# Decayed linear attention and a channel mix on one core: attention in sub-chunks of 64 tokens on 64x64 matmul tiles

## The chip, the cores and the metric

The kernel runs on one of the eight cores of a Trainium2 chip. The metric is the time of one execution on the device in microseconds (us). Before the change three runs gave 405.16, 406.31 and 408.67, median 406.31.

## The reference

Two layers follow each other, all in fp32. The first is linear attention with a decay for each feature, for 4 batches, 8 heads, 768 tokens and 48 features a head. The second is a channel mix: it blends each token with the one before, squares a ReLU, and multiplies by a sigmoid gate.

```python
for t in range(S):                       # attention, for every batch and head
    state = alpha[t, :, None] * state + outer(k[t], v[t])     # 48 x 48
    y[t] = q[t] @ state
x = y of all heads side by side          # 768 tokens x 384 features a batch
xk = mu_k * x + (1 - mu_k) * x_prev      # x_prev: the token before
xr = mu_r * x + (1 - mu_r) * x_prev
out = sigmoid(xr @ w_r) * (max(xk @ w_k, 0) ** 2 @ w_v)       # 384 -> 1024 -> 384
```

## The kernel before

**Groups and chunks.** The 3072 tokens are cut into chunks of 128 (`C`) and the chunks into nine groups: three groups of two chunks for batch 0, then two of three for each later batch. Heads go in four pairs (`NP`); a pair has its features on partitions 0 to 47 and 64 to 111. The decay is taken out of the recurrence: `prep_p` (line 227) runs the products of alpha as a scan (`pp`), and `prep_gh` (line 243) multiplies `q` by them, scans alpha backwards (`al`, line 254), and multiplies `k` by that. What is left is causal attention without decay: inside a chunk a masked product, across chunks a state of 48x48 a head.

**Attention of a chunk** (`attn`, line 281) is a list of pieces, each with a weight. For each pair, `scores` (line 318) makes k times q for the two heads of 128 tokens by 128, two matmuls on 48 partitions each; VectorE multiplies all eight by the mask into `am` (line 329, 1024 columns). `trans` (line 339) transposes k, ScalarE copies it out (`ht`). `both` runs `intra` (v times `am`, lines 384 and 391, two matmuls with 64 and 48 output partitions for a pair) and `update` (line 349, the state's growth, 48x48 for each head), and `inter` (line 407, old state times q, one 112x112 block-diagonal matmul a pair) adds to the same PSUM tile. The new state is the old one plus `pu` (line 357). ScalarE copies the outputs to `xt` and those of the last pair to `x3` (lines 416, 417), and two DMAs (line 420) spread them over the 16 free partitions beside each of the other three pairs' heads. Group 0 does without these DMAs (`direct`, line 403).

**The channel mix of a group**: `mix` (lines 460 to 470) makes xk and xr and splits each into a high part that a float32r matmul takes whole and a low rest. `moe` has three stages: up (line 487, 72 matmuls of three kinds: high times high, high times low, low times high), gate (line 512), and down (line 527). After up, ScalarE and VectorE make the ReLU, its square and the square's low part (lines 495 to 501). The weights are split in the same way while the first groups run (`split`).

**The order of work.** The streams of TensorE and SyncE are written out by hand; those of the other engines follow a scheduler's estimate and are then fixed. `merge` (line 46) puts the pieces of the next group's attention between the matmuls of this group's channel mix, by weight, so that the attention ends about 12 units (`LEAD`) before the mix does. A piece with no work (`pad`, `sp`) only spaces the others. In the first two groups, `PARAM["pos"]` says at which piece each weight split and each `prep` is issued, and 19 pieces of the attention of group 1 go ahead of the first up matmuls.

## Time and profile before

| what | value |
|---|---|
| three runs, median | 405.16, 406.31, 408.67; 406.31 us |
| the profiled execution, first to last instruction | 407.4 us |
| mean granted TensorE clock | 0.955 |
| busy: TensorE, VectorE, ScalarE, GpSimd | 371.3, 284.6, 190.8, 69.7 us |
| matmul records | 2834 |
| first up matmul of group 0 | 40.7 us |
| first up matmul of group 2 | 106.4 us |
| first up matmul of group 8, the last | 370.2 us |

The engines are PE (TensorE's matmuls), PEld (its weight loads), DVE (VectorE), ACT (ScalarE), POOL (GpSimd) and SP (SyncE). An fp32 matmul leaves two records, each with a weight load of its own; a float32r matmul and a transpose leave one. A stage below is the time from the first up matmul of a group to that of the next one: it holds the group's channel mix and the next group's attention.

### The profile page before, as it was taken

How to read it: one execution, taken by the hardware profiler on the slowest of the kernel's cores; microseconds unless marked ns; L12 is line 12 of the kernel's file. 1: busy time of each engine (PE TensorE's matmuls, PEld its weight loads, DVE VectorE, ACT ScalarE, POOL GpSimd, SP SyncE). 2: the span in 40 equal slices, each digit the busy share in tenths (PEclk: the TensorE clock that was granted, in tenths of full speed). 3: DMA queues.
4: the chain of work that ended last, by engine and by line, in shares of the span. 5: the costliest groups of instructions: out<-in, count | busy, mean ns of one | idle time of the engine just before them, and what ended most of it. 6: DMA issues, size and time to landing. Idle time of an engine off the chain costs nothing. (4 is left out here: it accounts for less than half of the span.)

```text
span 407.4 us, 7186 instructions
## 1 busy us (share of the span) xinstructions
PE 371.3 (91%) x2834; PEld 337.1 (83%) x2834; DVE 284.6 (70%) x451; ACT 190.8 (47%) x421; POOL 69.7 (17%) x85
## 2 busy tenths in 40 slices
PE   7665988898889999999989999999999999999993
PEld 6545877788779878898869978899889978999992
DVE  5899999995995699529972399809982654337510
ACT  3457864545644573327433273526634634345500
POOL 5364374250030004000400004000400000000000
PEclk9695998699999999999969999999999999999998
DMA  8994188336016212251023410251000100011001
GB/s 214 284 392 176 24 250 223 105 102 180 30 45 196 59 39 70 71 165 42 2 68 114 125 39 2 69 150 43 18 2 12 43 21 0 2 36 39 2 20 45
DMA packets 15816, 35.82 MB, mean 88 GB/s; under 512 B 1568, under 2 KB 9440, under 8 KB 15776
## 3 DMA queue, kind: packets, MB, share of 16 engines
q1 hardware_dynamic: 14608, 34.21, 27.7%
q10 hardware_dynamic: 1168, 1.09, 1.1%
q8 instruction: 24, 0.39, 0.4%
q14 instruction: 16, 0.13, 0.1%
HBM read 29.49 MB, written 4.72 MB: 84 GB/s over the span
## 5 line engine op out<-in xcount | busy, mean ns | idle before, releaser
L495 ACT ACTIVATE r<-pk 128x384 f32<-128x384 f32 (+1 forms) x72 | 32.2, 452 | 79.9 <-PE pk L487 49.1
L527 PE MATMUL pv<-wvl,kh 128*128 128x384 f32 x192 | 65.5, 341 | 2.9 <-DVE wvl L195 2.9
L527 PE MATMUL pv<-wvh,kl 128*128 128x384 f32 x192 | 65.6, 341 | 1.2 <-DVE kl L501 1.2
L527 PE MATMUL pv<-wvh,kh 128*128 128x384 f32 x192 | 65.2, 339 | 0.0
L318 PE MATMUL sp<-q,k 48*128 48x128 f32 x384 | 43.9, 332 | 18.4 <-DVE am L329 12.1
L318 PEld LDWEIGHTS sp<-q,k 48*128 48x128 f32 x384 | 29.8, 204 | 34.6 <-DVE am L329 14.6
L487 PE MATMUL pk<-xkh,wkh 128*128 128x384 f32 (+1 forms) x216 | 50.1, 339 | 2.1 <-ACT xkh L468 1.8
L487 PE MATMUL pk<-xkh,wkl 128*128 128x384 f32 (+1 forms) x216 | 50.0, 341 | 0.0
L501 DVE TENSOR_TENSOR kl<-k,kh 128x384 fp32r<-128x384 f32 (+1 forms) x72 | 45.7, 635 | 6.1 <-ACT kh L500 2.0
L487 PE MATMUL pk<-xkl,wkh 128*128 128x384 f32 (+1 forms) x216 | 49.5, 338 | 0.0
L460 ACT ACTIVATE x<-xt,mu 128x384 f32<-128x384 f32 (+1 forms) x54 | 29.4, 576 | 29.2 <-DMA xt<-x 21.6
L499 DVE TENSOR_TENSOR k<-r 128x384 f32<-128x384 f32 (+1 forms) x56 | 29.9, 534 | 17.8 <-ACT r L495 16.3
L254 DVE TENSOR_TENSOR_SCAN al<-al 112x383 f32<-112x383 f32 (+1 forms) x36 | 41.3, 1185 | 0.3
L249 DVE TENSOR_TENSOR q<-q,pp 112x768 f32<-112x768 f32 (+1 forms) x20 | 16.1, 808 | 36.3 <-DMA q<-q_p 36.3
L257 POOL TENSOR_TENSOR k<-k,al 112x768 f32<-112x768 f32 (+1 forms) x18 | 30.7, 1704 | 62.5 <-DVE al L254 46.1
L487 PEld LDWEIGHTS pk<-xkh,wkh 128*128 128x128 f32 x216 | 35.5, 195 | 4.9 <-ACT xkh L468 2.3
L527 PEld LDWEIGHTS pv<-wvl,kh 128*128 128x128 f32 x192 | 36.6, 190 | 3.2 <-DVE wvl L195 3.2
L527 PEld LDWEIGHTS pv<-wvh,kl 128*128 128x128 f32 x192 | 36.5, 190 | 1.8 <-DVE kl L501 1.8
L487 PEld LDWEIGHTS pk<-xkl,wkh 128*128 128x128 f32 x216 | 35.6, 194 | 2.8 <-issue 0.6
L487 PEld LDWEIGHTS pk<-xkh,wkl 128*128 128x128 f32 x216 | 35.2, 194 | 2.7 <-issue 0.2
L527 PEld LDWEIGHTS pv<-wvh,kh 128*128 128x128 f32 x192 | 36.6, 191 | 0.2 <-ACT wvh L192 0.2
L532 DVE TENSOR_TENSOR sig<-pv,sig 128x384 f32<-128x384 f32 x24 | 13.3, 554 | 33.3 <-ACT x L460 16.7
(93 smaller groups left out, 591.9 us busy)
## 6 DMA issues: line engine op xcount, KB each, us to landing
out<-sig SPq DMA_DIRECT2D x24, 192.0 KB, 1.8
k<-k_p SPq DMA_DIRECT2D x6, 672.0 KB, 4.6
al<-al_p SPq DMA_DIRECT2D x6, 672.0 KB, 4.8
q<-q_p SPq DMA_DIRECT2D x6, 672.0 KB, 6.6
v<-v_p SPq DMA_DIRECT2D x6, 672.0 KB, 5.3
wkraw<-wk_p SPq DMA_DIRECT2D x4, 768.0 KB, 14.2
vraw<-wv_p SPq DMA_DIRECT2D x4, 768.0 KB, 8.7
v<-v_p SPq DMA_DIRECT2D x3, 448.0 KB, 8.3
```

The lines of the kernel that those rows point to most:

```text
L249: (DVE if PARAM["g"][min(g, 2)][p] == "D" else POOL).tensor_tensor(q[:, hp], q[:, hp], pp[:, hp], op=ALU.mult)
L254: DVE.tensor_tensor_scan(back, back, back, initial=al[:, i, n : n + 1], op0=ALU.mult, op1=ALU.bypass)
L257: (DVE if PARAM["h"][min(g, 2)][p] == "D" else POOL).tensor_tensor(k[:, hp], k[:, hp], al[:, hp, 1:], op=ALU.mult)
L318: PE.matmul(sp[c][:, j, p, :], h[r0 : r0 + D, p, c * C : (c + 1) * C], q[r0 : r0 + D, p, c * C : (c + 1) * C], start=True, stop=True,)
L460: ACT.activation(x, xt[:, t, 1 : 1 + n], AF.Copy, scale=mu[:, i, t : t + 1])
L487: PE.matmul(pk, w[:, t, cols], x[:, t], start=part == 0 and t == 0, stop=part == 2 and t == NT - 1,)
L495: ACT.activation(r, pk, AF.Relu)
L499: DVE.tensor_tensor(k2, r, r, op=ALU.mult)
L501: DVE.tensor_tensor(kl[:, f], k2, kh[:, f].bitcast(F32), op=ALU.subtract)
L527: PE.matmul(pv, x[:, f, cols], w[:, f], start=f == 0 and i == 0, stop=f == NF - 1 and i == 2,)
L532: DVE.tensor_tensor(sig[t], pv, sig[t], op=ALU.mult)
```

## The change

Each chunk of 128 tokens is cut into two sub-chunks of 64 (`s`), and the state is kept at the start of each. Every product of the attention becomes a matmul with at most 64 partitions in and at most 64 out, so that it takes one quarter of the 128x128 array, and four neighbours in the stream always take the four different quarters:

- `scores`: 16 matmuls of 64 tokens by 64 (before 8 of 128 by 128); the mask has 512 columns instead of 1024.
- `intra`: 16 of 64 by 64 (before 8).
- `inter`: 16 (before 4). Those that land in the quarter's own half go to `yu`; the others (`cross`) go to `sp`, and `leave` adds them on VectorE (two adds of 128 columns a chunk, new).
- `update`: 16 with 48 columns (before 8). VectorE makes two states a chunk (`advance`, 192 columns each; before one state in two halves).

All of a chunk that can go together is one uninterrupted run (`visit`): the update of the next chunk, intra and inter of this one, and the scores of the next. A group of three chunks has four visits: update and scores; twice all four; intra and inter. The transposes stay separate pieces, ahead of each visit. `sp` and `yu` are single PSUM tiles of two banks each. The state is dense (192 columns) and goes round five buffers. The product with the carried scale is on VectorE for all groups (before on GpSimd for the first two). Group 0 uses the two DMAs as well. The table of positions becomes a short list (`FILL`), and the attention of group 1 goes wholly beside the channel mix of group 0. `prep` of a later group goes to the start of the attention's pieces. The layout of `v` on the host loses its padding, and the order of heads in the output is permuted with the weights.

The diff, cut to its core (what it removes of `attn` is in the listing above):

```diff
+HC = C // 2
+VW = H * D + HB - D
...
+PAD = 3.0
...
+FILL = [
+    ("wr0", 2), ("pp1", 4), ("wr1", 6), ("prep10", 8), ("prep11", 9), ("wv0", 11),
+    ("prep12", 13), ("prep13", 14), ("wv1", 17), ("load2", 18), ("wv2", 24), ("wv3", 28), ("pp2", 32),
+    ("prep20", 34), ("prep21", 36), ("prep22", 38), ("prep23", 40),
+]
...
+    none, *rings = (cp.tile([R, NP * D + HB - D], F32, name=f"st{i}") for i in range(5))
...
-        v = p2.tile([C, nck, NP, R], F32, tag="v", name=f"v{g}")
+        v = p2.tile([C, nck, VW], F32, tag="v", name=f"v{g}")
...
+        xt = p2.tile([128, NT + 1, 1 + n], F32, tag="xt", name=f"xt{g}")
...
+        sides = [(s, j) for s in range(2) for j in range(2)]
+        quads = [(o, j) for o in range(2) for j in range(2)]
...
+        def trans(c):
+            pt = ps.tile([C, NP, R], F32, tag="pt", name=f"pt{g}_{c}")
+            for p in range(NP):
+                need(f"prep{g}{p}")
+                PE.transpose(pt[:, p, :], h[:, p, c * C : (c + 1) * C], ident[:R, :R])
+            ht[c] = p2.tile([C, NP, R], F32, tag="ht", name=f"ht{g}_{c}")
+            ACT.copy(ht[c], pt)
+
+        def scores(c):
+            for p in range(NP):
+                need(f"prep{g}{p}")
+                for s, j in sides:
+                    rr = slice(j * HB, j * HB + D)
+                    t0 = c * C + s * HC
+                    PE.matmul(
+                        sp[c - 1][s * HC : (s + 1) * HC, j, p * HC : (p + 1) * HC],
+                        h[rr, p, t0 : t0 + HC], q[rr, p, t0 : t0 + HC],
+                        start=True, stop=True,
+                    )
+            am[c] = p2.tile([C, 2, NP, HC], F32, tag="am", name=f"am{g}_{c}")
+            DVE.tensor_tensor(
+                am[c], sp[c - 1][:, :, : NP * HC].rearrange("c j (p t) -> c j p t", p=NP),
+                mask.unsqueeze(1).unsqueeze(1).to_broadcast([C, 2, NP, HC]), op=ALU.mult,
+            )
+
+        def intra(c, opened):
+            for a in range(2):
+                for j in range(2):
+                    for s in range(2):
+                        for o in range(2):
+                            p = 2 * a + o
+                            e0 = (2 * p + j) * D
+                            i = 2 * a + j
+                            PE.matmul(
+                                yu[c][o * HB : (o + 1) * HB, s, i * HC : (i + 1) * HC],
+                                v[s * HC : (s + 1) * HC, c, e0 : e0 + HB],
+                                am[c][s * HC : (s + 1) * HC, j, p, :],
+                                start=i == 0 and s not in opened, stop=False, skip_group_check=True,
+                            )
+
+        def inter(c, cross):
+            for a in range(2):
+                for o, j in quads:
+                    p, s, i = 2 * a + o, j ^ cross, 2 * a + j
+                    rr = slice(j * HB, j * HB + D)
+                    t0 = c * C + s * HC
+                    oo = slice(o * HB, o * HB + (HB if cross else D))
+                    if cross:
+                        out_ = sp[c][oo, j, (NP + a) * HC : (NP + a + 1) * HC]
+                    else:
+                        out_ = yu[c][oo, s, i * HC : (i + 1) * HC]
+                    PE.matmul(
+                        out_, before[c, s][rr, p * D : p * D + (HB if cross else D)], q[rr, p, t0 : t0 + HC],
+                        start=bool(cross), stop=True, skip_group_check=True,
+                    )
+
+        def grown(c):
+            return yu[c - 1][:, :, NP * HC : NP * (HC + D)].rearrange("r s (p e) -> r s p e", p=NP)
+
+        def update(c, opened):
+            u = grown(c)
+            for p in range(NP):
+                for s, j in sides:
+                    if s not in opened:
+                        continue
+                    e0 = (2 * p + j) * D
+                    r0, r1 = j * HB, HB + j * D
+                    PE.matmul(
+                        u[r0:r1, s, p, :],
+                        ht[c][s * HC : (s + 1) * HC, p, r0:r1],
+                        v[s * HC : (s + 1) * HC, c, e0 : e0 + D],
+                        start=p == 0, stop=True, skip_group_check=True,
+                    )
+
+        def advance(c):
+            u = grown(c)
+            old = state.get(b, none)
+            before[c, 0] = old
+            new = before[c, 1] = fresh()
+            DVE.tensor_tensor(by_pair(new), by_pair(old), u[:R, 0], op=ALU.add)
+            if final and c == nck - 1:
+                return
+            nxt = state[b] = fresh()
+            DVE.tensor_tensor(by_pair(nxt), by_pair(new), u[:R, 1], op=ALU.add)
+            if c == nck - 1:
+                DVE.tensor_tensor(
+                    by_pair(nxt), by_pair(nxt),
+                    pscl[:R, g * NP : (g + 1) * NP].unsqueeze(2).to_broadcast([R, NP, D]),
+                    op=ALU.mult,
+                )
+
+        def leave(c):
+            x = xt[:, :, 1 + c * C : 1 + (c + 1) * C]
+            ACT.copy(
+                x[:R].rearrange("r i (s t) -> r i s t", s=2),
+                yu[c][:R, :, : NP * HC].rearrange("r s (i t) -> r i s t", i=NP),
+            )
+            for s in range(2):
+                part = x[:R, 1 - s :: 2, s * HC : (s + 1) * HC]
+                DVE.tensor_tensor(
+                    part, part,
+                    sp[c][:R, 1 - s, NP * HC : (NP + 2) * HC].rearrange("r (a t) -> r a t", a=2),
+                    op=ALU.add,
+                )
+            if c == nck - 1:
+                for o in range(2):
+                    (nc.sync if g == 0 else nc.scalar).dma_start(
+                        xt[o * HB + D : (o + 1) * HB, :NT, 1:], xt[o * HB : o * HB + D, NT, 1:]
+                    )
+
+        def visit(c):
+            more = c + 1 < nck
+            sp[c] = ps.tile([128, 2, 512], F32, tag="sp", name=f"sp{g}_{c}")
+            yu[c] = ps.tile([128, 2, 512], F32, tag="yu", name=f"yu{g}_{c}")
+            opened = ()
+            if more:
+                opened = (0,) if final and c + 2 == nck else (0, 1)
+                update(c + 1, opened)
+            if c >= 0:
+                intra(c, opened)
+                inter(c, 0)
+                inter(c, 1)
+            if more:
+                scores(c + 1)
+                advance(c + 1)
+            if c >= 0:
+                leave(c)
+
+        pieces = [(0.0, start), (0.4, lambda: trans(0)), (PAD, lambda: None)]
+        for c in range(-1, nck):
+            if c >= 0 and c + 1 < nck:
+                pieces += [(PAD, lambda: None), (0.4, lambda c=c: trans(c + 1)), (PAD, lambda: None)]
+            elif c >= 0:
+                pieces += [(2 * PAD, lambda: None)]
+            pieces.append((1.2 + 1.2 * (0 <= c < nck - 1), lambda c=c: visit(c)))
+        return pieces
...
-        for _, f in tick(attn(0)):
+        for i, (_, f) in enumerate(attn(0)):
             f()
+            if i == 3:
+                need("wk0")
+        need("wk1")
...
-                    side.insert(int(len(side) * PA["prep"]), (0.0, lambda: prep(g + 2)))
+                    side.insert(1, (0.0, lambda: prep(g + 2)))
...
-                    for _, f in side[: PA["a1"]] + main[: PA["hold"]]:
+                    for _, f in main[:HOLD]:
                         f()
-                    main, side = main[PA["hold"] :], side[PA["a1"] :]
+                    main = main[HOLD:]
```

**TensorE, group 4's channel mix with the attention of group 5.** `pk` is up, `sp` scores, `pt` the transposes. Before, from the first up matmul:

```order
L487 MATMUL pk<-xkh,wkh 128x384 x3
L318 MATMUL sp_0_1981<-q_1545,k_1544 128x128 x4
L487 MATMUL pk<-xkh,wkl 128x384 x3
L318 MATMUL sp_0_1981<-q_1545,k_1544 128x128 x2
L487 MATMUL pk<-xkl,wkh 128x384 x3
L318 MATMUL sp_0_1981<-q_1545,k_1544 128x128 x2
L339 MATMUL pt_0_2004<-ident,k_1544 128x112
L487 MATMUL pk<-xkh,wkh 128x384 x3
L339 MATMUL pt_0_2004<-ident,k_1544 128x112 x3
L487 MATMUL pk<-xkh,wkl 128x384 x3
L487 MATMUL pk<-xkl,wkh 128x384 x3
L487 MATMUL pk<-xkh,wkh 128x384 x3
```

After, from the end of the second visit on:

```order
L346 MATMUL sp_0_2570<-q_1885,k_1884 64x64 x16
L500 MATMUL pk<-xkh,wkh 128x384 x3
L500 MATMUL pk<-xkh,wkl 128x384 x3
L500 MATMUL pk<-xkl,wkh 128x384 x3
L500 MATMUL pk<-xkh,wkh 128x384 x3
L500 MATMUL pk<-xkh,wkl 128x384 x3
L500 MATMUL pk<-xkl,wkh 128x384 x3
L336 MATMUL pt_2_2675<-ident,k_1884 128x112 x4
L500 MATMUL pk<-xkh,wkh 128x384 x3
L500 MATMUL pk<-xkh,wkl 128x384 x3
L500 MATMUL pk<-xkl,wkh 128x384 x3
L500 MATMUL pk<-xkh,wkh 128x384 x3
```

The scores stood in pieces of two or four matmuls between threes of up; now they come as one block of 16 at the end of a visit, and up runs unbroken but for the transposes until the next one.

**VectorE, in the same stage.** `am` is the mask, `k` and `kl` the square and its low part, `al` the backward scan for a later group, `st` the state, `xt` the adds of `leave`. Before, near the stage's start:

```order
L235 RECIPROCAL al_2414<-pp_2415 112x4
L329 TENSOR_TENSOR am_0_2002<-sp_0_1981,mask 128x1024
L499 TENSOR_TENSOR k_1995<-r 128x384
L254 SCALAR_TENSOR_TENSOR al_1971<-al_1971 112x383
L501 TENSOR_TENSOR kl<-k_1995,kh 128x384
L254 SCALAR_TENSOR_TENSOR al_1971<-al_1971 112x383 x3
L499 TENSOR_TENSOR k_2041<-r 128x384
L501 TENSOR_TENSOR kl<-k_2041,kh 128x384
L499 TENSOR_TENSOR k_2057<-r 128x384
L501 TENSOR_TENSOR kl<-k_2057,kh 128x384
L329 TENSOR_TENSOR am_1_2087<-sp_1_2062,mask 128x1024
```

After, around the last two visits:

```order
L411 TENSOR_TENSOR st_107<-st_106,yu_1_2703 112x192
L415 TENSOR_TENSOR st_104<-st_107,yu_1_2703 112x192
L417 TENSOR_TENSOR st_104<-st_104,pscl 112x192
L352 TENSOR_TENSOR am_2_2768<-sp_1_2702,mask 128x512
L431 TENSOR_TENSOR xt_2424<-xt_2424,sp_1_2702 112x2x64 x2
L512 TENSOR_TENSOR k_2783<-r 128x384
L281 SCALAR_TENSOR_TENSOR al_2985<-al_2985 112x383
L514 TENSOR_TENSOR kl<-k_2783,kh 128x384
L281 SCALAR_TENSOR_TENSOR al_2985<-al_2985 112x383 x3
L431 TENSOR_TENSOR xt_2424<-xt_2424,sp_2_2816 112x2x64 x2
L276 TENSOR_TENSOR q_2988<-q_2988,pp_2986 112x768
L545 TENSOR_TENSOR sig<-pv,sig 128x384
```

The four scans stood among the first masks and squares of the stage; now they stand after the last mask, ahead of the last visit's two adds into `xt`.

## Prediction on record

> **What bounds the kernel now.** I read the page's busy times first, then the windows cut at the first up matmul of each group, then the chain of waits inside a clean stage.
>
> ```profile
> PE 371.3 (91%) x2834; PEld 337.1 (83%) x2834; DVE 284.6 (70%) x451; ACT 190.8 (47%) x421; POOL 69.7 (17%) x85
> ```
>
> PE is busy 91% of the span, but the windows show two regimes. Columns: window, length, then busy time (instructions) of PE, PEld, DVE, ACT, POOL, the granted clock, DMA.
>
> ```profile
> 0.00:40.70 40.70, 26.40 (x252) 22.96 (x253) 34.06 (x50) 20.23 (x38) 20.86 (x38) 0.79 0.84 267
> 40.70:70.70 30.00, 25.45 (x186) 24.10 (x185) 29.75 (x45) 19.64 (x50) 15.44 (x13) 0.94 0.59 162
> 70.70:106.40 35.70, 32.61 (x239) 29.64 (x238) 30.83 (x51) 18.73 (x52) 8.99 (x10) 0.90 0.41 117
> 106.40:143.10 36.70, 33.07 (x313) 30.52 (x312) 27.77 (x49) 18.60 (x46) 5.44 (x6) 1.00 0.32 93
> 143.10:187.50 44.40, 44.06 (x332) 39.52 (x332) 32.40 (x49) 19.50 (x43) 4.60 (x5) 1.00 0.28 83
> 187.50:236.10 48.60, 46.97 (x345) 41.90 (x344) 32.05 (x49) 20.32 (x45) 5.41 (x6) 0.93 0.25 69
> 236.10:282.20 46.10, 44.44 (x333) 39.58 (x332) 34.37 (x56) 22.11 (x48) 4.59 (x5) 1.00 0.21 66
> 282.20:326.10 43.90, 43.90 (x344) 39.52 (x344) 29.91 (x49) 22.90 (x49) 4.36 (x3) 1.00 0.05 18
> 326.10:370.20 44.10, 44.10 (x334) 39.64 (x333) 21.74 (x39) 19.06 (x40) 0.00 (x0) 1.00 0.05 18
> 370.20:407.40 37.20, 30.32 (x174) 29.72 (x172) 11.69 (x23) 9.71 (x20) 0.00 (x0) 0.97 0.07 24
> ```
>
> Up to 106.4 DVE is busy 34.06 + 29.75 + 30.83 = 94.6 us: VectorE sets the pace there (preps, weight splits). From 143 on PE is the bound: in the eighth and ninth windows it never rests. What attention costs PE shows in the chain, start, length, line, records:
>
> ```profile
> 297.59 0.39 PE pt L339 x4
> ...
> 326.29 0.52 PE pk L487 x3
> 326.81 0.65 PE sp L318 x8
> 327.45 0.72 PE pk L487 x3
> 328.18 0.42 PE sp L318 x4
> 328.60 0.72 PE pk L487 x3
> ...
> 338.31 0.36 PE pu L349 x16
> ...
> 350.64 0.44 PE py L407 x4
> ...
> 370.32 12.48 PE pk L487 x72
> 382.80 0.53 PE pg L512 x3
> ...
> 383.44 4.44 PE pg L512 x24
> 387.88 12.65 PE pv L527 x72
> ```
>
> The last group, with no attention beside it, needs 12.48 + 0.53 + 4.44 + 12.65 = 30.1 us. The stage before it takes 44.1, so three chunks of attention cost 14.0 us of PE, 4.7 each.
>
> **The change, part by part.** *Streaming.* Two more pairs of scores (four records of 128 columns) cost 0.65 - 0.42 = 0.23 us, 0.058 a record; on the full array (L407) a record costs 0.44 / 4 = 0.11. So two matmuls on different halves of the rows do run together; the 48-column updates, on different halves of the output, cost 0.36 / 16 = 0.0225 a record, 0.045 a simultaneous pair. Four at once are not in this trace. The bounds: four together take what a pair takes, or only two go together. I take the first, since halving by rows and halving by columns both work fully here. A round of four records with 64 columns then lies between the pairs with 48 (0.045) and 128 (0.115): 0.059. A chunk has 32 rounds, 8 of the update at 0.045 and 24 at 0.059: 1.78 us (3.56 if only two go together).
>
> *Switching.* A lone pair of scores costs 0.42 and lengthens the next three up matmuls from 0.52 to 0.72; less its streaming, 0.42 + 0.20 - 0.23 = 0.39 us for going into the split array and back. Four visits pay it four times a stage, where scores alone paid it ten times.
>
> *Sum of a stage.* First visit (update, scores) 8 x 0.045 + 8 x 0.059 + 0.39 = 1.22; two middle ones 1.78 + 0.39 = 2.17; last 16 x 0.059 + 0.39 = 1.33; three transposes as now 0.39 each. Together 1.22 + 4.34 + 1.33 + 1.17 = 8.1 us in place of 14.0: **5.9 us a stage**, in the six stages from 106.4 to 370.2.
>
> *VectorE, ScalarE, the rest.* Rows by operation and shape (mean ns of one stands before the second bar):
>
> ```profile
> L329 DVE TENSOR_TENSOR am<-sp,mask 128x1024 f32<-128x1024 f32 x24 | 29.2, 1215 | 7.2 <-PE sp L318 7.0
> L231 DVE TENSOR_TENSOR_SCAN pp<-al,tiny 112x384 f32<-112x384 f32 x24 | 23.1, 970 | 0.0
> L532 DVE TENSOR_TENSOR sig<-pv,sig 128x384 f32<-128x384 f32 x24 | 13.3, 554 | 33.3 <-ACT x L460 16.7 <-PE pv L527 16.4
> L357 DVE TENSOR_TENSOR sbd<-sbd,pu 48x192 f32<-48x192 f32 x32 | 11.2, 350 | 8.6 <-PE pu L349 8.2
> L416 ACT COPY x<-py 112x128 f32<-112x128 f32 x22 | 5.6, 257 | 13.3 <-PE py L407 11.0 <-PE py L391 2.3
> ```
>
> The mask with 512 columns lies between 384 (554 ns) and 1024 (1215): 0.69, a saving of 0.53 a chunk. The states stay two operations of 192 columns (0.35). The two adds of 128 columns, not in this trace, cost between ACT's 0.26 and 0.35: I take 0.28, 0.56 a chunk. VectorE's load in a stage thus stays as it is (30 to 34 us), and the ScalarE copy of 512 columns replaces two of 384 and 128. The two DMAs of group 0, the smaller `v` and the GpSimd fills lie beside other work. PE's new need is 30.1 + 8.1 = 38.2 us a stage, so VectorE, the next bound, stays below it, but at 80 to 90%.
>
> *Up to 106.4: no gain.* Counted in the order up to the first low square of group 2, VectorE has six masks for seven (6 x 0.69 against 7 x 1.215: -4.4), four more state operations (+1.4), twelve adds (+3.4), two scalings from GpSimd (+0.7), three more backward scans (about +3) and two fewer forward ones (-1.9): +2.2 us. Against that, up starts earlier, because the attention of group 1 no longer goes ahead of it, which takes away some of the 11.8 us in which VectorE is idle (bounds: all of the 2.2 lost and a few us of waits, or 4 us won). I take 107.0 for 106.4.
>
> *Waits.* Before lost time in the window from 187.5:
>
> ```profile
> 205.47 0.71 PE L318 MATMUL sp<-q,k 48*128 48x128 f32 x8 [1.63 <-DVE am L329]
> ...
> 212.41 0.87 PE L349 MATMUL pu<-v,ht 128*48 128x48 f32 x16
> 213.20 1.07 PE L487 MATMUL pk<-xkh,wkh 128*128 128x384 f32 x3
> ```
> ```profile
> 196.31 4.07 DVE L254 TENSOR_TENSOR_SCAN al<-al 112x383 f32<-112x383 f32 x3
> ...
> 200.93 2.02 DVE L501 TENSOR_TENSOR kl<-k,kh 128x384 fp32r<-128x384 f32 x1
> ```
> ```profile
> 207.00:213.80 6.80, 6.80 (x48) 5.38 (x49) 4.67 (x9) 1.03 (x3) 0.00 (x0) 0.50 0.01 2
> ```
>
> The scans held the mask up, PE waited 1.63 us, and then the clock was 0.50 for 6.8 us (3.4 lost). The new order puts the scans behind the last mask, so this wait goes. What is late next: the last visit's adds into `xt` now follow four scans, and the DMAs and `mix` follow them. Between the last visit and the next up lie six gate and 72 down matmuls, some 13.6 us; before, from the last output to the third high part took 13.6 us in the slowest stage:
>
> ```profile
> 223.50 0.49 ACT L417 COPY xt<-py 112x384 f32<-112x384 f32 x1
> ...
> 236.55 0.52 ACT L468 ACTIVATE xkh<-x 128x384 fp32r<-128x384 f32 x1 [0.34 <-DVE x L465]
> ```
>
> So a microsecond or so is lost at some boundaries, and the first transposed copy of a stage queues behind the mix on ScalarE, with only nine up matmuls (1.6 us) between it and its visit. I add 1.0 us in the stage from 106.4, 1.3 in the next three, then 0.5 and 0.3.
>
> *Sum.* 107.0; 36.7 - 5.9 + 1.0 = 31.8; 44.4 - 5.9 + 1.3 = 39.8; twice 44.1 - 5.9 + 1.3 = 39.5 (these two lose their own waits, down to 44.1); 43.9 - 5.9 + 0.5 = 38.5; 44.1 - 5.9 + 0.3 = 38.5; the last 37.2. Together 371.8 where the profiled execution has 407.4, which is 1.1 above the median: 35.6 less than 406.3, **371 us**.
>
> **The rivals.** *An issue limit.* No record in this trace follows the one before closer on average than the updates' 0.0225 us. If that is a limit on records and not the 48 columns, a chunk's 128 records take 2.88 us instead of 1.78: +3.3 a stage, +20 in six, 391; less what waits ready in the queue, 388. Against it: at the 0.50 clock the same updates take 213.20 - 212.41 = 0.79 us where the chain has 0.36 at full clock: they stretch as columns would. The Trainium skill speaks for it: "TensorE: Matmul & The Clock Gate", section "Wait — 56ns, not 53.3ns?", puts a floor of about 25 ns under start-to-start however few the columns; by that a chunk would take 3.2 us, an estimate from the page, and the time would be about 394. The updates at 22.5 ns already lie under it.
>
> *Only two together.* Then a chunk takes 3.56 us, a stage 5.3 more, and nearly the whole gain is gone: 371 + 6 x 5.3, less waits that vanish, about 400. For it: no row shows more than two. The skill's "TensorEngine Tiling (Array Packing)", section "Available Configurations", counts 64x64 as four independent tiles; no run here shows it yet.
>
> *VectorE stops PE, and the clock drops: slower.* `sp` and `yu` are single, so each visit waits until mask, states and adds of the last one are through VectorE. A wait like the one above costs 1.63 + 3.4 = 5.0 us. The gain is about 36 us, so from eight such waits in six stages on it is lost; at ten the time is 371 + 50 = 421. For it: VectorE at up to 90%, and 0.69 + 0.70 + 0.56 = 1.95 us of its work between two visits that only 24 up matmuls (a third of 12.48) and 0.39 of transposes keep apart, 4.6 us. Against it: the order puts masks and states ahead of scans.
>
> **How the numbers follow.** Forecast 0.69 (357 to 383: VectorE's waits up or down by 1.5 us a stage, and the first part by 4); issue limit 0.17 at 388; two together 0.08 at 400, half of it within 1%; waits and clock 0.06 at 421. A measurement here tells about 1% from no change. Faster by over 1%: 0.69 + 0.17 + 0.04 = 0.90; within 1%: 0.04; slower: 0.06. The range goes from 357 past the issue limit to 392.
>
> **What would show it.** In the windows after: stages of 38 to 40 us where they had 44 to 49, the last still 37.2, and the first up of group 2 near 107. In the chain: a middle visit of about 2.2 us between up matmuls, with four records starting close together in each round of 0.06. Visits of 3 us mean the issue limit, of 4 us two together. Waits of PE for `am`, `st` or `xt` with clock 0.50 mean the third rival. The forecast is wrong if stages stay above 42 us, or if the first up of group 2 comes after 112.

## The result and the profile after

| | before | after |
|---|---|---|
| time, median (range) | 407.49 us (405.16 to 409.66) | 392.06 us (391.77 to 394.70) |
| span of the profiled execution | 407.4 us | 390.1 us |
| first up of group 1 / 2 / 3 | 70.7 / 106.4 / 143.1 us | 84.7 / 114.9 / 154.3 us |
| from the first up of group 3 to the end | 264.3 us | 235.8 us |

The ratio is 0.9628 (95% interval 0.9575 to 0.9681): faster by 3.7%, where the forecast had 8.7%. The last two rows of the table carry the story. The part that TensorE bounds became 28.5 us shorter (forecast for it: 371.8 - 107.0 - 31.8 = 233.0 us, measured 235.8). The part before it became 11.2 us longer, where the forecast had 4.3 us shorter.

The busy times of the page, and the windows cut at the first up of each group, as they were cut for the kernel before (window, length, then busy time of PE, PEld, DVE, ACT, POOL, granted clock, DMA share, GB/s):

```profile
PE 332.0 (85%) x4590; PEld 315.5 (81%) x4590; DVE 281.6 (72%) x513; ACT 188.7 (48%) x393; POOL 65.3 (17%) x84
```
```profile
0.00:35.00 35.00, 17.04 (x308) 15.09 (x308) 24.82 (x42) 14.27 (x22) 15.30 (x36) 0.68 0.86 247
35.00:84.70 49.70, 32.40 (x402) 30.19 (x402) 47.99 (x73) 26.34 (x62) 24.24 (x20) 0.81 0.55 163
84.70:114.90 30.20, 27.84 (x386) 26.49 (x387) 20.73 (x45) 19.30 (x51) 1.34 (x4) 0.90 0.33 99
114.90:154.30 39.40, 32.25 (x536) 30.10 (x536) 29.69 (x58) 16.84 (x39) 7.05 (x7) 0.91 0.32 88
154.30:195.30 41.00, 38.63 (x553) 36.63 (x552) 34.33 (x60) 20.00 (x41) 7.19 (x6) 1.00 0.35 98
195.30:236.10 40.80, 38.20 (x569) 36.44 (x568) 32.15 (x60) 20.66 (x42) 5.43 (x6) 1.00 0.24 69
236.10:277.90 41.80, 39.60 (x552) 37.91 (x552) 34.22 (x65) 22.02 (x45) 4.54 (x5) 0.96 0.23 72
277.90:315.80 37.90, 37.90 (x568) 36.51 (x568) 24.53 (x51) 20.53 (x40) 0.19 (x1) 1.00 0.06 21
315.80:353.80 38.00, 38.00 (x554) 36.61 (x553) 21.96 (x46) 19.10 (x37) 0.00 (x0) 1.00 0.07 22
353.80:390.10 36.30, 30.10 (x174) 29.49 (x172) 11.23 (x22) 9.62 (x19) 0.00 (x0) 0.97 0.07 24
```

PE's busy time fell by 39 us, VectorE's by 3. The eighth and ninth windows, where PE never rests (the clean stages below, those of groups 6 and 7), went from 43.9 and 44.1 to 37.9 and 38.0. In the second window VectorE works 47.99 of 49.70 us and PE 32.40. Up to group 3's first up VectorE has about the same work in both kernels (before 34.06 + 29.75 + 30.83 + 27.77 = 122.4 us, after 24.82 + 47.99 + 20.73 + 29.69 = 123.2), but it idles 31.1 us in place of 20.7.

**A visit of the clean stages.** The chain from 284 us on (start, length, line, records):

```profile
284.48 0.39 PE pt L336 x4
284.87 1.58 PE pk L500 x9
286.45 0.55 PE yu L399 x23
...
287.71 0.29 PE sp L383 x16
288.00 0.47 PE sp L346 x32
288.46 3.32 PE pk L500 x18
```

The visit lasts from 286.45 to 288.46, 2.01 us (forecast 2.17). Its 32 score records take 0.47 us, 0.0147 each, 0.059 for a round of four. By the prediction's reading a record of 128 columns has the full array for 0.11 us, so one of 64 columns would need 0.055 (an estimate); 32 x 0.055 / 0.47 = 3.7 of them are at work at once.

**The start of group 1.** The last copy of group 1's outputs into `xt` and the first copy of its mix on ScalarE, before and then after:

```profile
59.83 0.48 ACT L417 COPY xt<-py 112x384 f32<-112x384 f32 x1
...
63.46 0.91 ACT L460 ACTIVATE x<-xt,mu 128x256 f32<-128x256 f32 x2 [0.21 <-DMA xt<-x]
```
```profile
69.84 0.57 ACT L425 COPY xt<-yu 112x512 f32<-112x512 f32 x1
...
71.01 3.62 DVE L258 TENSOR_TENSOR_SCAN pp<-al,tiny 112x384 f32<-112x384 f32 x3
...
74.56 0.45 DVE L431 TENSOR_TENSOR xt<-xt,sp 112x128 f32<-112x128 f32 x2
...
76.13 4.98 DVE L281 TENSOR_TENSOR_SCAN al<-al 112x383 f32<-112x383 f32 x4
...
78.89 0.91 ACT L478 ACTIVATE x<-xt,mu 128x256 f32<-128x256 f32 x2 [8.10 <-DMA xt<-xt]
...
81.48 2.32 DVE L276 TENSOR_TENSOR q<-q,pp 112x768 f32<-112x768 f32 x1
...
83.73 0.87 DVE L479 SCALAR_TENSOR_TENSOR x<-xt,nu,x 128x256 f32<-128x256 f32 x2
...
84.70 0.97 PE L500 MATMUL pk<-xkh,wkh 128*128 128x256 f32 x2 [9.28 <-ACT xkh L482]
```

After, the attention of group 1 ends 10 us later. Its last two adds stand behind scans of group 3 (the copy is done at 70.4, the adds run at 74.6), and the mix stands behind four more scans and a product (ScalarE's first `x` is there at 79.3, VectorE takes it at 83.7). TensorE, done with group 0 at 75.4, waits 9.28 us.

**Group 2's stage, and the next ones.** Waits of PE in the window from 114.9 to 154.3 (in all, times, longest; `ht` is the copy of the transposes, `kl` the low part of the square, `st` the state), and two stretches of it:

```profile
PE yu_-1_1414 L399 <- ACT ht L338: 2.5, 1, 2.5
PE pv L540 <- DVE kl L514: 2.3, 2, 1.8
PE yu L399 <- DVE st L415: 2.0, 1, 2.0
```
```profile
125.00:130.00 5.00, 4.57 (x131) 4.33 (x132) 4.42 (x10) 0.59 (x1) 0.80 (x3) 0.51 0.25 69
130.00:135.00 5.00, 5.00 (x147) 4.87 (x148) 2.57 (x8) 2.04 (x5) 0.00 (x0) 0.81 0.01 3
```

Three kinds of wait of about 2 us, and after the first two (they end at 119.4 and 125.2) a clock of 0.51 and 0.81, which over these 10 us costs 2.45 + 0.95 = 3.4 us. The third, for `kl` at 147.2 and 149.8, comes after VectorE has stood at the head of its queue for the transfer of `q`:

```profile
145.89 0.96 DVE L276 TENSOR_TENSOR q<-q,pp 112x768 f32<-112x768 f32 x1 [4.29 <-DMA q<-q_p]
```

At the start of group 5's stage only the first kind of wait is left, for the copy of the first transposes, behind the last parts of the mix on ScalarE:

```profile
240.57 0.51 ACT L338 COPY ht<-pt 128x448 f32<-128x448 f32 x1
...
241.13 0.99 PE L399 MATMUL yu_-1_3039<-v,ht 64*64 64x48 f32 x30 [2.20 <-ACT ht L338]
```

### The profile page after: what moved, and what is told of

The parts are those of the page before. It is cut to its first block, busy times and chain, and to the rows that moved or that the text cites. A ratio compares the mean times of both kernels' runs of the same rounds, so it can differ in the third digit from the quotient of the medians.

```text
span 390.1 us, 10751 instructions
## 1 busy us (share of the span) xinstructions
PE 332.0 (85%) x4590; PEld 315.5 (81%) x4590; DVE 281.6 (72%) x513; ACT 188.7 (48%) x393; POOL 65.3 (17%) x84
## 4 chain that ended last, share of the span: by engine, by line
PE 47%; DVE 20%; DMA 6%; issue 4%; ACT 3%; ACTq 0%; DVEq 0%
PE pk L500 19%; PE pv L540 13%; PE pg L525 5%; DVE al L281 4%; DMA xt<-xt 4%; DVE pp L258 4%; DVE x L479 3%; PE yu L365 2%; DMA q<-q_p 2%; DVE xkl L483 2%; DVE q L276 1%; PE pt L336 1%; DVE kl L514 1%; PE sp L346 1%; PE yu L399 1%
## 5 line engine op out<-in xcount | busy, mean ns | idle before, releaser
L500 PE MATMUL pk<-xkh,wkh 128*128 128x384 f32 (+1 forms) x216 | 51.4, 345 | 21.7 <-ACT xkh L482 21.7
L500 PEld LDWEIGHTS pk<-xkh,wkh 128*128 128x128 f32 x216 | 37.9, 203 | 24.5 <-ACT xkh L482 23.6
L284 POOL TENSOR_TENSOR k<-k,al 112x768 f32<-112x768 f32 (+1 forms) x18 | 31.1, 1733 | 91.3 <-DVE al L281 50.0
L478 ACT ACTIVATE x<-xt,mu 128x384 f32<-128x384 f32 (+1 forms) x54 | 28.5, 575 | 35.6 <-DMA xt<-xt 25.5
L514 DVE TENSOR_TENSOR kl<-k,kh 128x384 fp32r<-128x384 f32 (+1 forms) x72 | 36.7, 509 | 11.0 <-ACT kh L513 5.8
L281 DVE TENSOR_TENSOR_SCAN al<-al 112x383 f32<-112x383 f32 (+1 forms) x36 | 39.7, 1137 | 1.3 <-ACT junk L265 1.1
L500 PEld LDWEIGHTS pk<-xkl,wkh 128*128 128x128 f32 x216 | 38.4, 203 | 0.8 <-DVE xkl L483 0.3
L500 PEld LDWEIGHTS pk<-xkh,wkl 128*128 128x128 f32 x216 | 37.2, 202 | 0.9
L258 DVE TENSOR_TENSOR_SCAN pp<-al,tiny 112x384 f32<-112x384 f32 (+1 forms) x36 | 33.9, 963 | 4.2 <-DMA al<-al_p 4.2
L513 ACT ACTIVATE kh<-r 128x384 fp32r<-128x384 f32 (+1 forms) x72 | 34.7, 488 | 1.4
L479 DVE SCALAR_TENSOR_TENSOR x<-xt,nu,x 128x384 f32<-128x384 f32 (+1 forms) x54 | 31.9, 631 | 2.7 <-ACT x L478 2.7
L425 ACT COPY xt<-yu 112x512 f32<-112x512 f32 x24 | 14.1, 588 | 35.8 <-DVE st L415 25.3
```

The lines of the kernel that those rows point to most:

```text
L258: DVE.tensor_tensor_scan(pp[:, p], al[:, p, :n], tiny[:R].to_broadcast([R, n]), initial=START, op0=ALU.mult, op1=ALU.max,)
L281: DVE.tensor_tensor_scan(back, back, back, initial=al[:, i, n : n + 1], op0=ALU.mult, op1=ALU.bypass)
L284: (DVE if QH[min(g, 2)][p] == "D" else POOL).tensor_tensor(k[:, hp], k[:, hp], al[:, hp, 1:], op=ALU.mult)
L478: ACT.activation(x, xt[:, t, 1 : 1 + n], AF.Copy, scale=mu[:, i, t : t + 1])
L479: DVE.scalar_tensor_tensor(x, xt[:, t, 0:n], nu[:, i, t : t + 1], x, op0=ALU.mult, op1=ALU.add)
L500: PE.matmul(pk, w[:, t, cols], x[:, t], start=part == 0 and t == 0, stop=part == 2 and t == NT - 1,)
```

## The experiments

All times beside the kernel before, run on the same chip (its medians there were 407.4 to 409.1 us); kernels on different chips are compared by their ratios. "Up 1" and "up 3" are the first up matmuls of groups 1 and 3 in the profiled execution.

| kernel | made from | us | ratio to before (95%) | up 1 | up 3 |
|---|---|---|---|---|---|
| after | | 392.06 | 0.9628 (0.9575 to 0.9681) | 84.7 | 154.3 |
| d_pairs | after | 401.98 | 0.9831 (0.9777 to 0.9885) | 85.4 | 155.4 |
| s_split | after | 397.25 | 0.9740 (0.9680 to 0.9799) | 84.1 | 158.1 |
| b_prep3 | after | 393.79 | 0.9644 (0.9583 to 0.9705) | 78.3 | 155.1 |
| a_first | after | 385.64 | 0.9440 (0.9374 to 0.9505) | 78.7 | 149.2 |
| e_twice | after | 403.04 | 0.9862 (0.9803 to 0.9922) | 83.0 | 163.8 |
| e_none | after | 382.96 | 0.9359 (0.9313 to 0.9406) | 80.8 | 146.2 |
| j_a0 | before | 416.95 | 1.0223 (1.0143 to 1.0303) | 79.2 | 152.5 |
| j_prep | before | 427.24 | 1.0513 (1.0423 to 1.0603) | 70.9 | 160.6 |
| c_qpool | after | 405.04 | 0.9946 (0.9907 to 0.9986) | 83.2 | 156.3 |
| g_lateq | a_first | 420.32 | 1.0295 (1.0234 to 1.0355) | 78.6 | 148.1 |
| f_ht | a_first | 382.21 | 0.9363 (0.9294 to 0.9433) | 78.3 | 149.6 |
| h_ht3 | a_first | 379.51 | 0.9279 (0.9230 to 0.9327) | 79.7 | 149.8 |
| h_cast | h_ht3 | 380.21 | 0.9297 (0.9253 to 0.9340) | 81.0 | 150.0 |
| h_some | h_ht3 | 378.56 | 0.9256 (0.9215 to 0.9298) | 79.9 | 147.9 |

### What a visit costs

**d_pairs: two quarters at a time.** In `scores`, `intra`, `inter` and `update` alike, as here in `scores`:

```
-                for s, j in sides:
+            for two in (((0, 0), (1, 1)), ((0, 1), (1, 0))):
+                for p, (s, j) in ((p, t) for p in range(NP) for t in two):
```

Expected: 

> The same matmuls of a visit in another order: first all that use two diagonal quarters of the array, then all that use the other two, so that only two quarters can be at work at once. Theory of the forecast (four quarters together): a middle visit grows from about 2.0 us by as much again less its switching, to 3.6-4.0 us; three chunks a stage make the clean stages (38.0 us) 43 to 44, and the whole 410-425 us. Rival (only two ever worked together, and the gain comes from fewer visits alone): a visit stays at 2.0 us and the whole at 392. Rival (an issue limit sets 15 ns a record whatever the quarters): also 2.0 us and 392.

Measured: 402 us, clean stages of 39.6 in place of 38.0, and a middle visit from 291.91 to 294.44, 2.53 us:

```profile
291.91 0.70 PE yu L400 x21
...
293.84 0.60 PE sp L347 x26
294.44 3.33 PE pk L501 x18
```

The number of matmuls and of visits is the same, and the visit grew from 2.01 to 2.53 us. So more than two quarters do work together in the changed kernel, and no limit on records hides it: both rivals fall. But the visit did not grow to the 3.6 to 4.0 us that the theory had, nor the clean stages to 43. At its end, among scores alone, a record takes 0.60 / 26 = 0.023 us in place of 0.0147. Elsewhere records of the next two quarters start while the first two still run: records of `inter` (line 384 of this kernel) start at 293.00 us, ahead of records of `intra` (line 366) at 293.04 to 293.16, which come before them in the program. So the order of the program does not hold TensorE to two.

**s_split: three more visits a stage.**

```
-            pieces.append((1.2 + 1.2 * (0 <= c < nck - 1), lambda c=c: visit(c)))
+            w = 0.6 + 0.6 * (0 <= c < nck - 1)
+            pieces += [(w + 1.0 * (c >= 0), lambda c=c: former(c)), (w, lambda c=c: latter(c))]
```

(`former` holds `update` and `intra`, `latter` the rest of `visit`.) Expected: 

> The changed kernel with each visit that has outputs cut in two, the updates and products with the masks ahead of some up or gate matmuls, the products with the states and the next scores behind them: three more visits a stage. By the forecast's price of a visit (0.39 us for going into the split array and back) the stages without waits grow from 38.0 to 39.2 us; by what the trace of the changed kernel shows (38.0 less 30.1, less transposes 0.95 and three chunks of 1.86 us leaves about 0.3-0.4 us a stage for four visits) they grow by 0.3-0.6, to 38.3-38.6. In the earlier stages a cut gives VectorE a little longer for states and masks, at most a few tenths won. The whole 392-400.

Measured: the two clean stages take 39.0 us each; the second:

```profile
319.80:358.80 39.00, 39.00 (x553) 36.66 (x552) 21.88 (x46) 19.28 (x38) 0.00 (x0) 1.00 0.06 21
```

That is 1.0 us for three visits, 0.34 each: the forecast's 0.39 is nearly right. The smaller price in the expectation was a slip: 38.0 - 30.1 - 0.95 - 3 x 1.86 leaves 1.4 us for four visits, 0.34 for each, and not 0.3 to 0.4 for all four. With it the clean stage adds up: 30.1 + 3 x 1.78 + 4 x 0.34 + 3 x 0.39 = 38.0.

### What made the first part longer

**b_prep3: group 3's preparation behind group 1's mix.**

```
+        low = tiny
+        if g == 3:
+            low = p2.tile([128, 1], F32, tag="low", name=f"low{g}")
+            POOL.tensor_scalar(
+                low, xs[g - 2][3][:, NT - 1, 0:1].bitcast(F32), 0.0, FLOOR, op0=ALU.mult, op1=ALU.add
+            )
...
-                pp[:, p], al[:, p, :n], tiny[:R].to_broadcast([R, n]), initial=START,
+                pp[:, p], al[:, p, :n], low[:R].to_broadcast([R, n]), initial=START,
```

Expected: 

> The four forward scans of group 3 read their floor from a small tile that GpSimd writes only when the mix of group 1 has been computed, so the whole preparation of group 3 (about 12 us of VectorE) comes behind that mix instead of ahead of it. Theory A (the 15 us were lost because preparation of later groups stands ahead of the mix on VectorE): the first up matmul of group 1 moves from 84.7 to 75-78 us, right behind the last down matmul of group 0 (75.4). What is given back later: the 12 us now stand ahead of the first masks of the next stage, so that stage gets longer than its 30.2 us; the whole takes 384 to 390 us against 392. Theory B (the loss comes from the attention of group 1 lying beside group 0's channel mix, whatever the preparations do): the first up of group 1 stays at 82 or later and the time at 391-393. Theory C (the xt transfers are late): the same, 82 or later.

Measured: the first up of group 1 comes at 78.3, as theory A has it, with 0.34 us of wait left, and nothing of it is kept:

```profile
34.90:78.30 43.40, 34.17 (x403) 31.53 (x403) 36.16 (x63) 26.27 (x62) 16.29 (x15) 0.78 0.63 186
78.30:118.40 40.10, 30.82 (x386) 29.28 (x387) 31.26 (x55) 19.30 (x51) 8.01 (x10) 0.83 0.26 76
```

VectorE's 12 us moved from the second window (47.99 to 36.16) into the third (20.73 to 31.26), which grew from 30.2 to 40.1. So the 9.28 us of wait, the largest of the trace, was where the loss showed, not what caused it.

**a_first: group 1's attention ahead again.**

```
-                    for _, f in main[:HOLD]:
+                    for _, f in side[:8] + main[:HOLD]:
...
-                    main = main[HOLD:]
+                    main, side = main[HOLD:], side[8:]
```

Expected: 

> The attention of group 1 up to its second visit goes ahead of group 0's up matmuls again, as in the kernel before; everything else is as after. Theory B (the place of the attention of group 1): the first up of group 0 goes from 35.0 back to 40-43 us, the first up of group 1 from 84.7 to 70-74 us, and the whole takes about 380. Theory A (preparations ahead of the mix): forward scans and a product of group 3, about 7 us of VectorE, still stand ahead of the mix of group 1, so its first up comes at 78 or later and the whole takes 386-394.

Measured: 385.6 us. The first up of group 0 goes back to 44.0, that of group 1 comes at 78.7 (still behind scans of group 3, 5.4 us after group 0's last matmul), that of group 3 at 149.2. This is 5.1 us of the 11.2. The first up of group 1 is as theory A had it (78 or later) and the whole 0.4 us under its range; theory B's 70 to 74 and 380 did not come.

**e_twice and e_none: more and less work for VectorE.** The forward scans of groups 2 to 8 twice, and the backward scans of groups 2 to 4 left out:

```
-        for p in range(p0, p0 + m):
+        for p in sorted([*range(p0, p0 + m)] * (1 + (g > 1))):
```
```
-            for i in range(p, p + st):
+            for i in range(p, p + st) if g not in (2, 3, 4) else ():
```

Expected of e_twice: 

> The changed kernel with the four forward scans of each group from group 2 on made twice (the second writes the same numbers): 4 x 0.6 us more VectorE work for group 2 and 4 x 0.95 for each later one. Theory A (VectorE's work sets the end of the first part, up to group 3's first up matmul, and nothing after it): that first up moves from 154.3 by most of the 2.4 + 3.8 us of groups 2 and 3, to 158-161 (group 4's scans may lie in it too); each later stage grows by less than 0.5 us; the whole 396-400 against 392. Rival (no engine's work is the bound; single waits on transfers are): the extra scans fill idle time, the first up of group 3 stays within 2 us of 154.3, and the whole within 2 us of 392. Rival (VectorE bounds every stage): each of six stages grows by 3 us or more, the whole to 410.

Expected of e_none: 

> The changed kernel with the backward scans of alpha of groups 2, 3 and 4 left out, so their products with k use the raw alpha: 4 x 0.65 + 8 x 0.95 = about 10 us less VectorE work in the first part. Theory A (VectorE's work is the bound up to group 3's first up, in both directions): that first up moves from 154.3 to 144-147, the later stages stay as they are, the whole 381-385 against 392. Rival (waits on transfers and on the order set a floor just under): the first up stays above 150, the whole above 387.

Measured: group 3's first up at 163.8 and at 146.2, where it was 154.3 (e_twice past its forecast of 158 to 161, e_none within its 144 to 147). The two windows up to it, of e_twice and then of e_none:

```profile
0.00:119.90 119.90, 82.74 (x1096) 76.83 (x1097) 101.47 (x171) 59.72 (x132) 40.31 (x60) 0.76 0.57 165
119.90:163.80 43.90, 34.82 (x536) 32.81 (x535) 34.81 (x63) 18.01 (x42) 6.96 (x7) 0.84 0.28 80
```
```profile
0.00:112.80 112.80, 79.84 (x1097) 73.84 (x1097) 85.31 (x152) 59.95 (x133) 40.67 (x61) 0.77 0.63 180
112.80:146.20 33.40, 30.08 (x535) 28.56 (x535) 23.48 (x52) 16.43 (x38) 3.61 (x5) 0.95 0.27 83
```

VectorE's busy time there is 136.3 and 108.8 us in place of 123.2: 13.1 us more cost 9.5, 14.4 us less bring 8.1. The stages of groups 4 to 7 move by at most 0.4 us under e_twice (group 3's by 2.6). So the first part depends on VectorE's work, and little behind it does. Over the whole part it does so at 0.56 to 0.73 us for each us of work. The two windows differ: up to group 2's first up, 7.9 us more work cost 5.0 and 8.2 less bring 2.1, so much of that stretch is waits; in group 2's stage, 5.1 more cost 4.5 and 6.2 less bring 6.0, nearly one for one.

**j_a0 and j_prep: the two edits of order alone, in the kernel before.**

For j_a0, in `PARAM`, `'a1': 19` becomes `'a1': 0`, so that none of the 19 pieces goes ahead. For j_prep:

```
-                    side.insert(int(len(side) * PA["prep"]), (0.0, lambda: prep(g + 2)))
+                    side.insert(1, (0.0, lambda: prep(g + 2)))
```

Expected of j_a0: 

> The kernel before, with its old attention, but none of group 1's attention ahead of group 0's up matmuls (19 pieces of it stood there). Theory B (the order of the start costs the time, whatever the attention's form): the first up of group 0 comes at about 35 instead of 40.7, that of group 3 at 148-154 instead of 143.1, the whole 412-418 us against 407. Rival (the new form of the attention costs it: more and later VectorE operations): the first up of group 3 stays within 2 us of 143.1 and the whole at 405-409.

Expected of j_prep: 

> The kernel before with the preparations of the group after next put at the start of each stage's attention instead of a fifth into it, as in the change. VectorE's order around the first masks of groups 3 to 8 then changes: four backward scans come before the mix's end or behind it rather than among the masks. Theory: the wait that stood in the stage from 187.5 us (1.6 us and the clock's fall, 5 us together) goes in this order, and the stage takes 44 instead of 48.6; first part within 2 us of 143.1; the whole 402-406. Rival (the preparations then hold up the first visits): slower, 408-412.

Measured, j_a0: 417 us, and group 3's first up at 152.5 in place of 143.1. From there on it needs 264.3 us, to the tenth what the kernel before needs. The rows of the start of group 1, and the windows:

```profile
66.54 0.50 ACT L417 COPY xt<-py 112x384 f32<-112x384 f32 x1
...
75.35 0.91 ACT L460 ACTIVATE x<-xt,mu 128x256 f32<-128x256 f32 x2 [8.31 <-DMA xt<-x]
```
```profile
0.00:35.10 35.10, 19.45 (x177) 17.52 (x177) 27.85 (x41) 14.48 (x28) 18.63 (x37) 0.80 0.95 295
35.10:79.20 44.10, 35.17 (x259) 32.22 (x259) 41.45 (x58) 24.28 (x58) 20.30 (x17) 0.85 0.45 131
```

With the old attention throughout, putting none of group 1's attention ahead costs 9.4 us: group 0's up comes at 35 as in the changed kernel, group 1's outputs 6.7 us later than before, its mix 11.9 us later. So this order can make the first part longer without any 64x64 tile. It does not do so in the same place, though. Here the two transfers into `xt` take 7.5 us to land (medians of the profile's transfers; 2.9 in the kernel before, 3.5 in the changed one), and ScalarE waits 8.31 us for them, while in the changed kernel scans on VectorE hold up the last adds and the mix. That the two kernels lose about as much (9.4 and 11.2 us) is thus not shown to be one cause; in the changed kernel itself this order is worth the 5.1 us of a_first.

j_prep came out on the side of its rival, and beyond: 427 us, 17.5 us of it up to group 3's first up. VectorE then makes scans and products ahead of the masks in the second and third stages (waits of PE in the window from 70 to 207):

```profile
PE sp L318 <- DVE am L329: 12.8, 3, 7.2
```
```profile
70.90:113.70 42.80, 35.81 (x240) 32.80 (x239) 32.12 (x52) 19.42 (x52) 7.93 (x11) 0.80 0.35 101
113.70:160.60 46.90, 37.52 (x312) 34.62 (x311) 31.23 (x50) 18.39 (x45) 7.20 (x7) 0.85 0.26 72
```

The changed kernel has this edit too. The same wait, of visits for the mask, is only 2.6 us there between 35.0 and 154.3 us (15.9 in j_prep up to group 3's first up); the changed kernel without the edit was not run.

**h_cast: five casts from VectorE to ScalarE** (made from h_ht3, below).

```
-    "wr": ("DP", "DP"),
-    "wv": ("DP", "DP", "AD", "DP"),
+    "wr": ("AP", "AP"),
+    "wv": ("AP", "AP", "AD", "AP"),
```

Expected: 

> h_ht3, and five casts of high weight parts (0.47 us each) go from VectorE to ScalarE, which was busy 19-20 us of each 33-35 us there. Theory A (VectorE's work sets the end of the first part): 2.3 us less work, the first up of group 3 at 146.5-147.5 instead of 149.2, the whole 377-379. Rival (ScalarE's queue, in which the parts of the mix stand, gives it back): within 1 us of h_ht3.

Measured: 380.2 us beside 379.5, first up of group 0 at 45.0 and of group 3 at 150.0: no gain. Work that ScalarE takes over at this point is not won.

### The waits at the boundaries

**c_qpool: the products of q on GpSimd.**

```
-QG = ("PDDD", "DPDP", "DDDP")
+QG = ("PDDD", "DPDP", "PPPP")
```

Expected: 

> From group 2 on the two products of q with the forward products of alpha go to GpSimd instead of VectorE, so VectorE no longer waits for the q transfer at the head of its queue (4.3 us before group 3's mix) and has 1.7 us less to do a stage; GpSimd gets two more products of some 2 us beside VectorE. Theory C (late transfers at the head of VectorE's queue cost time at the boundaries): the first up of group 3 comes 3-4 us earlier than 154.3 against that of group 2, the whole 386-389. Theory A alone: preparations of later groups only fill the gap, so the whole stays within 3 us of 392. Rival: GpSimd's products slow VectorE beside them by as much as they take away: 391-394.

Measured: 405 us, outside all three ranges. Group 2's stage does become shorter, 34.5 us for 39.4, which is the sign that theory C gave; but group 1's takes 38.5 for 30.2, so that group 3's first up comes 2.0 us later, and the stages of groups 3 to 5 take 44 to 45 us. At the start of one of them:

```profile
195.26 3.66 POOL L276 TENSOR_TENSOR q<-q,pp 112x768 f32<-112x768 f32 x2 [3.38 <-DMA q<-q_p]
...
198.95 0.96 DVE L258 TENSOR_TENSOR_SCAN pp<-al,tiny 112x384 f32<-112x384 f32 x1 [5.19 <-POOL q L276]
...
204.72 0.45 PE L500 MATMUL pk<-xkh,wkh 128*128 128x384 f32 x1 [2.72 <-ACT xkh L482]
```

`pp` has one buffer. Its next scan overwrites what GpSimd's product still reads, and it stands ahead of the mix on VectorE: VectorE now waits 5.19 us for GpSimd, which waits for the transfer. The wait at the head of the queue was not taken away: at this boundary it was 5.15 us, for the transfer itself, in the changed kernel, and at the one before it grew from 4.29 to 6.34.

**g_lateq: the products of q behind the first part of the mix** (made from a_first; a tile `one`, made from the last `xkl`, is a factor of each product, and the product in its old place is left out from group 3 on).

```
+        DVE.tensor_scalar(
+            one, xs[g - 1][1][:, NT - 1, 0:1].bitcast(F32), 0.0, 1.0, op0=ALU.mult, op1=ALU.add
+        )
...
+            DVE.scalar_tensor_tensor(q[:, hp], q[:, hp], one[:R], pp[:, hp], op0=ALU.mult, op1=ALU.mult)
```

Expected: 

> On top of a_first (385.6 us): from group 3 on, the two products of q with the forward products of alpha read a one that VectorE writes once the low part for up has been computed, so they come behind that part of the mix instead of ahead of it, and VectorE doesn't stand waiting for the q transfer (4.4 us before group 3's mix, 2.0 us before group 2's). Theory C (that wait at the head of VectorE's queue lengthens group 2's stage, 37.1 us where its matmuls need some 27): that stage takes 33-35 us, the first up of group 3 comes at 145-147 instead of 149.2, the whole 381-384. Rival (the preparations that then bunch behind the mix hold up the first visit of the next stage): the gain in group 2's stage is given back in group 3's; the whole 385-388.

Measured: 420 us. Group 2's stage takes 38.1 us (37.1 in a_first): nothing is won there. Scans and products then bunch behind the mix, and in four stages a visit waits for the states (waits of PE from 148 to 341 us; the first two of these stages):

```profile
PE yu L412 <- DVE st L428: 30.0, 4, 7.7
```
```profile
148.10:197.90 49.80, 40.55 (x553) 38.89 (x552) 34.25 (x61) 21.80 (x44) 5.04 (x6) 0.90 0.23 70
197.90:246.10 48.20, 40.42 (x570) 38.89 (x569) 34.00 (x60) 20.72 (x42) 4.90 (x5) 0.89 0.25 73
```

This is the third rival of the forecast, made to happen: VectorE stops PE once a stage for 7.5 us, the mean clock of the stage is 0.9, and the stages take 48 to 50 us though VectorE has no more work in them (34 us).

**f_ht and h_ht3: the first transposes ahead of the mix** (made from a_first; in h_ht3 for groups 5 to 8 alone).

```
+    def ahead(g):
+        early[g] = attn(g)
+        early[g].pop(1)[1]()
...
-                side = attn(g + 1)
+                side = early.pop(g + 1, None) or attn(g + 1)
...
+                    main.insert(len(main) - 14, (0.0, lambda: ahead(g + 2)))
```

Expected of f_ht: 

> On top of a_first (385.6 us): the first transposes of each group from group 3 on, and ScalarE's copy of them, are taken ahead of the mix in the stage before, 14 pieces of gate and down matmuls ahead of its end, instead of beginning the stage. Theory (in the stages from 149 to 271 us TensorE loses its 2 us to the copy that queues behind the mix on ScalarE, the wait of 1.8 to 2.5 us that the trace shows at each stage's first update): these waits go, the stages from groups 3, 4 and 5 take 38.2-38.8 us instead of 40.6-41.0, group 2's some 2 us less as well, the whole 377-380. Rival (the wait then goes to the states and masks, which stand behind the same mix on VectorE): the stages stay at 40 or more, the whole at 384-386.

Expected of h_ht3: 

> f_ht with the early transposes for groups 5 to 8 alone: for groups 3 and 4 TensorE stood up to 6.2 us at them, waiting for GpSimd's product of k. Theory (the copy behind the mix costs 2 us a stage wherever k is ready in time): the first up of group 3 comes at 149.2 as in a_first, group 3's stage stays at 41, those of groups 4 and 5 take 38.2, and the whole 379.5-381.5 against a_first's 385.6. Rival (what f_ht gained in those stages hung on its slower ones before): stages of 40 again, 385.

Measured, f_ht: 382.2 us; the stages of groups 4 and 5 take 38.3 and 38.2 (40.7 and 40.6 in a_first), that of group 3 takes 41.8 (41.0 there), and that of group 2 is not 2 us shorter, as expected, but longer (38.6 for 37.1). h_ht3: 379.5 us, and for groups 4 and 5

```profile
189.90:228.10 38.20, 38.19 (x569) 36.49 (x568) 31.57 (x59) 20.37 (x42) 5.51 (x6) 1.00 0.26 73
228.10:266.20 38.10, 38.10 (x552) 36.45 (x551) 32.84 (x63) 20.61 (x43) 4.24 (x5) 1.00 0.24 74
```

PE no longer rests in the stages of groups 4 and 5: the one wait that was left there was that copy. What the expectation of h_ht3 says of the 6.2 us is wrong: the same wait for GpSimd's `k` is in h_ht3's trace, so it does not come from the early transposes of groups 3 and 4. The intervals of f_ht overlap with those of a_first and of h_ht3; those of a_first and h_ht3 lie apart.

**h_some: h_ht3 with one visit of group 1's attention ahead** (`side[:4]` in place of `side[:8]`). Expected: 

> h_ht3 with only the first visit of group 1's attention ahead of group 0's up matmuls, the other two beside its channel mix. Theory A: VectorE's order until group 1's mix is nearly that of a_first, so the first up of group 3 stays within 2 us of 149.2 and the whole within 2 us of h_ht3. Theory B (the place of that attention decides): half of the 5 us between the changed kernel and a_first come back, the first up of group 3 at 151-152, the whole 382-384.

Measured: 378.6 us, group 3's first up at 147.9. One visit ahead is as good as two. This is the lowest time of the versions, though not clear of h_ht3 and h_cast: 7.4% under the kernel before and 3.9% under the changed one (0.9256 / 0.9628; these two intervals lie apart).

## Why the prediction was wrong in size and right in kind

**Streaming: right.** A round of four score records takes 0.059 us as forecast, from the chain above. The issue limit falls: 0.0147 us a record is below the 0.0225 on which that rival stood. The Trainium skill's page "TensorE: Matmul & The Clock Gate", section "Wait — 56ns, not 53.3ns?", has about 25 ns as the least from start to start; this trace disagrees, and the measurement decides (on any one quarter the records are 0.058 us apart, so that for a single tile the page is not put to the test here). "Only two together" falls by d_pairs; here the trace agrees with the Trainium skill's "TensorEngine Tiling (Array Packing)", section "The Solution", which counts four independent 64x64 tiles.

**Switching: right.** 0.34 us a visit by s_split, forecast 0.39.

**The sum of a stage: right where PE is the bound.** The forecast of 8.1 us of attention in place of 14.0 compares with 37.9 - 30.1 = 7.8. Stages 3 to 8 of the sum:

| stage of group | 3 | 4 | 5 | 6 | 7 | 8 |
|---|---|---|---|---|---|---|
| forecast | 39.8 | 39.5 | 39.5 | 38.5 | 38.5 | 37.2 |
| measured | 41.0 | 40.8 | 41.8 | 37.9 | 38.0 | 36.3 |

**Waits: the places right, one price too small.** The wait behind the scans from 205 us is gone, and the copy of the first transposes did queue behind the mix on ScalarE. It cost 2.4 us a stage (40.7 against 38.3 without it) where the forecast had 1.3.

**"Up to 106.4: no gain": wrong, the step that failed.** The forecast's count of VectorE's work is not what failed: it had 2.2 us more up to group 2's first low square, and by the windows there are 1.1 us less up to group 2's first up and 0.8 more up to group 3's. It then said that up starts earlier and that this "takes away some of the 11.8 us in which VectorE is idle". The opposite happened: up to group 2's first up VectorE idles 21.4 us. With none of group 1's attention ahead, its outputs, its mix and so its up come late; meanwhile VectorE runs ahead with preparations of groups 2 and 3, and lacks that work afterwards (20.73 of 30.20 us busy in the third window). Group 2's first up comes at 114.9 for 107.0, past the 112 that the prediction itself had named as a sign of being wrong. j_a0 shows that this order can cost 9.4 us without any of the new tiles; in the changed kernel, a_first and h_some bring 5.1 and 6.4 of the 11.2 us back, about half. What the other half hangs on stays open. I had counted work and not followed the chain attention, transfer, mix, up of one group through the new order.

**"36.7 - 5.9 + 1.0 = 31.8": wrong as well.** The stage of group 2 takes 39.4 us. I had put it with the six stages that PE bounds, though its up, gate and down are two thirds of the others' and VectorE had 27.8 us to do in it. It is bounded by VectorE: with more work for VectorE it takes 43.9 us (e_twice), with less 33.4 (e_none), 0.9 to 1.0 us for each us of that work. What PE saves there comes back as waits, one of them for `st` with the clock at 0.51 and 0.81 after it: the third rival's sign, in this one stage.

The two steps are 7.9 + 7.6 = 15.5 of the 18.3 us between the forecast's 371.8 and the span of 390.1; the other 2.8 are the stages of groups 3 to 5 (+4.8: the waits for the copy, and in group 5's a clock of 0.96) less the last three stages (-2.0).

**What stays open.** h_some still reaches group 3 at 147.9, 4.8 us after the kernel before, with less work for VectorE (28.56 + 36.15 + 25.11 + 28.88 = 118.7 us against 122.4, from its windows). Which waits of the first part hold the rest was not settled. The place of `prep`, which cost so much in j_prep, was not put back in the changed kernel, and the other edits of the start (the list `FILL`, the scale's product on VectorE, the DMAs of group 0) were not run alone; each may hold a part of it. A third buffer for q, which would let its transfer come earlier, was not tried.

## What to carry to other kernels

A change that saves time on one engine is worth that only in the stages that this engine bounds: cut the trace by stage, and leave out of the sum each stage that another engine bounds. A busy share does not tell which: in group 2's stage VectorE was busy for 29.7 of 39.4 us, and yet nearly every microsecond added to its work or taken from it showed in the time. Where a change also moves work in the order of the start, follow the dependent chain of one group (its attention, transfer, mix, first matmul) through the new order; equal amounts of work say nothing on when it can be done. The longest wait in a trace need not be its cause: b_prep3 took 9 us of it away and won nothing, since the work that stood there had to be done in the next stage.

## What the runs showed of the hardware that was not expected

- Matmul records of 64 columns on the four quarters follow each other every 0.0147 us on average (32 records in 0.47 us).
- TensorE does not keep to two quarters because neighbouring matmuls use only two: in d_pairs a visit takes 2.53 us, where strict pairs would need 3.56 us of streaming alone, and records of `inter` start ahead of records of `intra` (293.00 and 293.04 us) that come before them in the program.
- With a wait of PE of 7.5 us once a stage the mean granted clock of the whole stage is 0.9 (g_lateq). Two waits of 2.5 and 2.0 us, which end 6 us apart, are followed by 5 us at 0.51 and 5 at 0.81 (group 2's stage after the change). A single wait of 2.2 us left the clock at 1.00 in group 4's stage, and was followed by 6.5 us at 0.74 in group 5's; what decides between the two is not shown.
